# Casts, transfer order, working tiles and output queue in the opening of a linear-attention and mixer kernel

## The chip, the cores and the metric

The kernel runs on one core of a Trainium2 chip. A core has TensorE (PE, matrix multiply, with its weight loads shown as PEld), VectorE (DVE), ScalarE (ACT), GpSimd (POOL) and SyncE (SP), each with its own instruction stream, and 16 DMA engines. In this kernel SP and POOL issue the DMAs. The metric is the device time of one execution in microseconds; before the change its median over three runs is 300.36 us (299.21 to 301.64). One execution is also recorded by the hardware profiler; its times, counted from the start of its span, are the profile's.

## What is computed

Linear attention (elu + 1 feature map) over 8 batches of 8 heads, 576 tokens and 64 dimensions, and then an MLP mixer over tokens and channels on its result:

```python
def phi(x):
    return np.where(x > 0, x, np.exp(x) - 1.0) + 1.0
q_p, k_p = (phi(q), phi(k))                       # q, k, v: (8, 8, 576, 64) fp32
kv = np.einsum('bhsd,bhse->bhde', k_p, v)
z = np.sum(k_p, axis=2)
num = np.einsum('bhsd,bhde->bhse', q_p, kv)
den = np.einsum('bhsd,bhd->bhs', q_p, z)[..., None] + 1e-06
attn = num / den

x = attn.transpose(0, 2, 1, 3).reshape(8, 576, 512)
xt = x.transpose(0, 2, 1)
h = np.maximum(xt @ w_tok1, 0.0) @ w_tok2         # 576 -> 256 -> 576
u = x + h.transpose(0, 2, 1)
h2 = np.maximum(u @ w_ch1, 0.0) @ w_ch2           # 512 -> 1536 -> 512
out = u + h2                                      # (8, 576, 512) fp32
```

## The kernel before

**Tiling.** Of a batch's 576 tokens, 512 lie as 4 per partition on 128 partitions (index r = 0 to 3), and the last 64, the tail, as a fifth slot (r = 4) on half of the partitions: the lower half for even batches, the upper for odd ones. Two batches make a pair, so that one matmul of the channel mixer can take the tails of both. Heads come in two groups g of four. Inputs are loaded in fp32 into `*_raw` tiles, one set for even and one for odd batches.

**Steps of a batch.** `phi` makes phi(x) as max(min(exp(x), 1), x + 1): `phi_exp` on ACT (line 114), `phi_add` on DVE (line 120), and `phi_end` on DVE (lines 128 and 129) into `kp` or `qp`. `vcast` turns v to bf16 into `vs`, whose 65th column per head is one, so that `kv` (line 165) yields k'v and the sum of k' together; ACT copies these into `kvbd`. `qtr` transposes q' on PE (line 175), and ACT copies it into `qT`. `nd` multiplies both (line 196) and DVE divides into `x` (lines 206 to 209). `mm1` (line 231) and `mm2` (line 242) are the token mixer, DVE adds x to give `u` (line 248, the tail on line 246), `utr` transposes u (line 259). `mm3` (line 332) is the first channel matmul, 12 pieces of four matmuls, each followed by relu on ACT into `cr` (line 336), and `mm4` (line 355) the second, per tile t of tokens (0 to 3 and 4 to 7 of the pair's two batches, 8 for both tails), followed by an add on DVE into an output buffer (line 361) and a store (line 364). For batch 0 there are versions in two column halves (`mm1_first`, `mm2_first`, `utr_first`). `warm` issues matmuls of the identity whose result nobody reads.

**Order.** The schedule is by hand: each engine runs its instructions in the order in which the program issues them, and waits for data where it must. Buffers: a pool tile with `bufs=n` waits for its n-th predecessor's readers; `ps_big` has four PSUM banks, `ps_sm` two tiles of two banks, `outp` three output buffers, `work` two of each. After the opening, `run(bigs, fill)` walks through a list of big steps (mm3 and mm4 pieces of batch n) and after big step i issues the fill steps with number i (preparation of batches n+1 and n+2). Batch 0's mm4 (`m4_0`) goes through all four token tiles for each of the 12 slices kc of w_ch2, so w_ch2 is read slice by slice while its four slabs (three slices each) arrive.

**Transfers.** SP issues all loads of q, k, v and all stores. POOL issues the weights, which are converted to bf16 on the way: w_tok1 (`w1`, tail rows `w1t`), w_tok2 (`w2`), w_ch1 in four slabs (`wc1`, line 412) and w_ch2 in four slabs (`wc2`, line 417). `after(dma, other)` lets a DMA wait on its issuing engine until another has landed: w_tok1 waits for batch 0's last q, batch 1's k for the second w_ch1 slab, w_ch2's first slab for batch 1's first v, its second for batch 1's first q, and batch 2's k for w_ch2's third slab. Line numbers of the profile are those of the kernel before.

## Time and profile before

| | |
|---|---|
| median of 3 runs (lowest, highest) | 300.36 us (299.21, 301.64) |
| the profiled execution: its time, its span | 302.12 us, 300.3 us |
| granted TensorE clock, mean of the span | 0.988 |
| PE busy | 277.8 us (92%) |
| PEld busy (overlaps PE) | 158.5 us (53%) |
| DVE busy | 166.9 us (56%) |
| ACT busy | 167.4 us (56%) |
| POOL busy | 14.0 us (5%) |
| DMA | 41.84 MB, mean 139 GB/s |

A busy time is the time in which an engine executes; the span is the time from the first to the last event. An engine can be busy for a small share of the span and still decide it in one stage, so the views used below go by time: a table of busy times by stretch of the span, the timeline of instructions (with the idle time ahead of each and what ended it, in brackets), groups of instructions by line, and the chain of waits that ends last.

### The profile page before, as it was taken

To read this page: it belongs to the slowest core of one execution; us is meant where nothing else is said; L and a number is where in the kernel's file an instruction comes from. 1 tells how busy PE (TensorE), PEld (TensorE's weight loads), DVE (VectorE), ACT (ScalarE), POOL (GpSimd) and SP (SyncE) were. 2 spreads that over 40 slices of the span, in tenths; PEclk is the share of its full clock that TensorE was granted. 3 is DMA by queue.
4 is the path that set the end of the run, shared out by engine and by line. 5 is a ranking of instruction groups with operands and counts; after the bars stand their busy time and mean duration, and the time that the engine had idled before them with its cause. 6 is when DMAs were issued, how large, how long until landed. Compare 5 with 4: busy or idle time off the path is not lost.

```text
span 300.3 us, 5077 instructions
## 1 busy us (share of the span) xinstructions
PE 277.8 (92%) x1992; PEld 158.5 (53%) x1992; DVE 166.9 (56%) x324; ACT 167.4 (56%) x258; POOL 14.0 (5%) x24
## 2 busy tenths in 40 slices
PE   8968867976899989999999999999999999999994
PEld 8956324533374446545656455455565465454641
DVE  5794345646456794779276815595658617340021
ACT  3642688212997458655877437845797076126500
POOL 3190040000000000000000000000000000000000
PEclk9989999997999999999999999999999999999999
DMA  7969999997997595097308650011000210011022
GB/s 202 269 90 201 311 226 152 275 303 226 288 292 212 170 268 175 2 258 244 113 3 244 223 179 0 0 71 71 1 3 35 101 41 2 35 71 37 0 78 97
DMA packets 47959, 41.84 MB, mean 139 GB/s; under 512 B 14656, under 2 KB 43200, under 8 KB 47936
## 3 DMA queue, kind: packets, MB, share of 16 engines
q1 hardware_dynamic: 43648, 37.76, 43.3%
q0 software_dynamic: 4288, 3.77, 8.5%
q8 instruction: 15, 0.25, 0.3%
q14 instruction: 8, 0.07, 0.1%
HBM read 35.85 MB, written 9.44 MB: 151 GB/s over the span
## 4 chain that ended last, share of the span: by engine, by line
PE 70%; DMA 9%; ACT 7%; SPq 5%; DVE 3%; issue 2%; POOL 1%; ACTq 0%; DVEq 0%
PE h_ps L355 28%; PE c_ps L332 23%; PE a_ps L231 4%; PE h_ps L242 4%; SPq L105 3%; PE nd_ps L196 3%; PE c_ps L343 3%; DMA wc<-in_moe_w_ch_dram 3%; DMA v_raw<-in_v_dram 2%; PE tp L175 2%; ACT e L114 2%; PE tp L259 2%; SPq L103 2%; DMA q_raw<-in_q_dram 2%; PE kv_ps L165 2%
## 5 line engine op out<-in xcount | busy, mean ns | idle before, releaser
L332 PE MATMUL c_ps<-uT,wc 128*128 128x512 bf16 x384 | 93.8, 382 | 3.2 <-ACT cr L336 1.5
L355 PE MATMUL h_ps<-wc,cr 128*128 128x512 bf16 x384 | 90.4, 379 | 2.7 <-DMA wc<-in_moe_w_ch_dram 2.7
L336 ACT ACTIVATE cr<-c_ps 128x512 bf16<-128x512 f32 x96 | 56.8, 599 | 48.6 <-PE c_ps L332 48.4
L355 PEld LDWEIGHTS <-cr 128*128 128x128 bf16 x384 | 36.5, 98 | 42.5 <-DMA wc<-in_moe_w_ch_dram 3.2
L332 PEld LDWEIGHTS <-wc 128*128 128x128 bf16 x384 | 35.6, 98 | 37.2 <-issue 5.6
L128 DVE TENSOR_SCALAR e<-e 128x1280 bf16<-128x1280 bf16 (+1 forms) x34 | 17.0, 500 | 32.9 <-ACT e L114 32.9
L361 DVE TENSOR_TENSOR o_sb<-h_ps,u 128x512 f32<-128x512 f32 x32 | 21.8, 686 | 24.0 <-PE h_ps L355 20.0
L209 DVE TENSOR_TENSOR x<-nd_ps,den 128x512 bf16<-128x512 f32 (+1 forms) x48 | 28.9, 602 | 1.7
L206 DVE TENSOR_SCALAR den<-nd_ps 128x8 f32<-128x8 f32 (+1 forms) x48 | 7.8, 162 | 36.0 <-PE nd_ps L196 35.5
L263 ACT COPY uT<-tp 128x1024 bf16<-128x1024 bf16 x7 | 7.1, 1012 | 27.3 <-PE tp L259 27.3
L114 ACT ACTIVATE e<-k_raw 128x1280 bf16<-128x1280 f32 x16 | 20.3, 1270 | 3.4 <-DMA k_raw<-in_k_dram 3.3
L114 ACT ACTIVATE e<-q_raw 128x1280 bf16<-128x1280 f32 (+1 forms) x18 | 20.3, 1149 | 2.1 <-DMA q_raw<-in_q_dram 1.0
L196 PEld LDWEIGHTS <-qT 128*128 128x128 bf16 x160 | 13.0, 100 | 11.2 <-ACT qT L187 1.2
L187 ACT COPY qT<-tp 128x1280 bf16<-128x1280 bf16 x14 | 17.2, 1231 | 2.1 <-PE tp L175 2.1
L196 PE MATMUL nd_ps<-kvbd,qT 128*128 128x130 bf16 x160 | 17.4, 226 | 0.5 <-ACT qT L187 0.4
L248 DVE TENSOR_TENSOR u<-h_ps,x 128x1024 bf16<-128x1024 f32 x14 | 16.5, 1217 | 0.7 <-PE h_ps L242 0.7
L234 ACT ACTIVATE ar<-a_ps 128x512 bf16<-128x512 f32 x14 | 7.5, 592 | 15.7 <-PE a_ps L231 15.7
L242 PE MATMUL h_ps<-ar,w 128*128 128x512 bf16 x56 | 14.4, 379 | 0.8 <-ACT ar L234 0.7
L144 ACT CAST vs<-v_raw 128x1024 bf16<-128x1024 f32 x14 | 14.8, 1058 | 0.0
L385 PE MATMUL bank<-identity 128*128 128x128 bf16 x178 | 13.5, 247 | 1.4 <-POOL identity masks.py:199 1.4
L231 PE MATMUL a_ps<-x,w 128*128 128x512 bf16 x56 | 14.4, 379 | 0.0
L120 DVE TENSOR_SCALAR y<-k_raw 128x1280 bf16<-128x1280 f32 x16 | 13.2, 822 | 2.0 <-DMA k_raw<-in_k_dram 1.7
(76 smaller groups left out, 268.3 us busy)
## 6 DMA issues: line engine op xcount, KB each, us to landing
k_raw<-in_k_dram SPq DMA_DIRECT2D x16, 512.0 KB, 5.3
q_raw<-in_q_dram SPq DMA_DIRECT2D x16, 512.0 KB, 6.9
v_raw<-in_v_dram SPq DMA_DIRECT2D x16, 512.0 KB, 6.8
out_dram<-o_sb SPq DMA_DIRECT2D x32, 256.0 KB, 2.5
wc<-in_moe_w_ch_dram POOLq DMA_DIRECT2D x8, 384.0 KB, 8.0
k_raw<-in_k_dram SPq DMA_DIRECT2D x16, 64.0 KB, 5.2
q_raw<-in_q_dram SPq DMA_DIRECT2D x16, 64.0 KB, 6.5
v_raw<-in_v_dram SPq DMA_DIRECT2D x16, 64.0 KB, 6.4
```

What stands on the lines that cost most here:

```text
L114: nc.scalar.activation(out=e, in_=f, func=AF.Exp)
L128: nc.vector.tensor_scalar(out=e, in0=e, scalar1=1.0, scalar2=None, op0=ALU.min)
L187: nc.scalar.copy(out=qT[b][:, 2 * g:2 * g + 2].rearrange("p j r c -> p (j r) c"), in_=tp[:, 0:2 * R1])
L196: nc.tensor.matmul(out=ps[:, i, a * 2 * D1:(a + 1) * 2 * D1], lhsT=qT[b][:, j, r, :], rhs=kvbd[b][:, j, :], start=True, stop=True)
L209: nc.vector.tensor_tensor(out=x[b][:, rs[0]:rs[0] + m, HG * D * g:HG * D * (g + 1)].rearrange("p r (h d) -> p r h d", h=HG), in0=v_[:, :, ...
L231: nc.tensor.matmul(out=ps[:, mt], lhsT=w1t[:, b, ms] if r == R else w1[:, r, ms], rhs=x[b][:, r, :], start=(r == 0), stop=(r == R))
L242: nc.tensor.matmul(out=ps[:, i], lhsT=w2t[:, kt, b, :] if r == R else w2v[:, kt, r], rhs=ar[b][:, kt, :], start=(kt == 0), stop=(kt == NT ...
L248: nc.vector.tensor_tensor(out=u[b][:, rs[0]:rs[0] + m], in0=ps[:, 0:m], in1=x[b][:, rs[0]:rs[0] + m], op=ALU.add)
L332: nc.tensor.matmul(out=ps, lhsT=wc1[:, kj, 128 * mc:128 * mc + 128], rhs=uT[b][:, kj].rearrange("p r c -> p (r c)"), start=(kj == 0), stop ...
L336: nc.scalar.activation(out=cr[b][:, mc, :], in_=ps, func=AF.Relu)
L355: nc.tensor.matmul(out=ps, lhsT=crt[:, kc, :] if t == 8 else cr[b][:, kc, 128 * r:128 * r + 128], rhs=wc2[:, kc, :], start=(kc == 0), stop ...
L361: nc.vector.tensor_tensor(out=o, in0=ps, in1=ut[p % 2] if t == 8 else u[b][:, r, :], op=ALU.add)
```

## The change

- `vcast` of batch 0 runs on ACT and no longer on POOL; that of batch 1 runs on DVE.
- `kp`, `qp` and `vs` exist once and no longer for even and odd batches; v's tail slot becomes a tile of its own, `vst`, one for even and one for odd batches. `outp` has six buffers and the exponentials four.
- POOL's weight transfers follow w_tok1 at once. The second `w1t` part goes behind w_ch1, and w_ch2's first slab comes right behind that, without a wait; the other three wait for batch 1's last v. A wait on a load now means its main part, not its tail part.
- Stores go on POOL's queue, except those of the last pair, which stay on SP.
- In the opening both transposes of q of a head group go ahead of kv and nd (with copies on DVE for the first group); the fillers are placed anew (60, 20 of half width and 22 in the place of 130; 30 and 30 around a nd piece; some of 4 and 6). `mm2_first(1)` goes ahead of the first halves of mm3, of which there are two and no longer three.
- In batch 0's channel mixer `phi` of k is issued at steps 5 and 7 (8 and 9 before), `vcast` at 9 and 11 (11 and 12), kv at 11 (12), `phi` of q at 12 (14), the transposes at 14 and 15 (14 and 16), nd at 16 to 21 (17 to 22) and mm1 at 22 (23). The adds and stores of batch 0's four output tiles become `mm4_end`, issued after the sums u: the first ahead of `utr`, the others behind it.

The diff, cut to its core:

```diff
-    outp = ctx.enter_context(tc.tile_pool(name="outp", bufs=3))
+    outp = ctx.enter_context(tc.tile_pool(name="outp", bufs=6))
...
-    kp = [const(f"kp{b}", [128, R1, H, D]) for b in range(2)]
-    qp = [const(f"qp{b}", [128, R1, H, D]) for b in range(2)]
-    vs = [const(f"vs{b}", [128, R1, H, D1]) for b in range(2)]
+    kp = const("kp", [128, R1, H, D])
+    qp = const("qp", [128, R1, H, D])
+    vs = const("vs", [128, R, H, D1])
+    vst = [const(f"vst{b}", [128, H, D1]) for b in range(2)]
...
-        e = work.tile([128, HG * R1 * D], BF16, name="e", tag="e")[:, :nh * R1 * D]
+        e = work.tile([128, HG * R1 * D], BF16, name="e", tag="e", bufs=4)[:, :nh * R1 * D]
...
-    def vcast(n, g, eng=None):
+    def vcast(n, g, copy=nc.scalar.copy):
         b = n % 2
         hs = slice(HG * g, HG * g + HG)
-        dst = vs[b][:, 0:R, hs, 0:D].transpose([0, 2, 1, 3])
-        if eng is None:
-            nc.scalar.copy(out=dst, in_=raw["v", b][:, hs, 0:R])
-        else:
-            eng.tensor_copy(out=dst, in_=raw["v", b][:, hs, 0:R])
-        nc.scalar.copy(out=vs[b][half[b], R, hs, 0:D], in_=raw["v", b][half[b], hs, R])
+        copy(out=vs[:, :, hs, 0:D].transpose([0, 2, 1, 3]), in_=raw["v", b][:, hs, 0:R])
+        copy(out=vst[b][half[b], hs, 0:D], in_=raw["v", b][half[b], hs, R])
...
-        if put:
+        if put == "act":
             nc.scalar.copy(out=qT[b][:, j], in_=tp[:, 0:R1])
+        elif put == "dve":
+            nc.vector.tensor_copy(out=qT[b][:, j], in_=tp[:, 0:R1])
...
+    def mm4_end(p, t):
+        ps = held[t]
+        b, r = divmod(t, R)
         o = outp.tile([128, DM], FP32, name="o_sb", tag="o_sb")
         nc.vector.tensor_tensor(out=o, in0=ps, in1=ut[p % 2] if t == 8 else u[b][:, r, :],
                                 op=ALU.add)
+        put = nc.sync if p == B // 2 - 1 else nc.gpsimd
         if t < 8:
-            nc.sync.dma_start(
+            put.dma_start(
...
+    def warm_half(m):
+        ps = bank()
+        for i in range(m):
+            h = half[i % 2]
+            nc.tensor.matmul(out=ps[h, 0:D1], lhsT=identity[:, h], rhs=identity[:, 0:D1],
+                             start=True, stop=True)
...
     phi("k", 0, 0, HG)
-    warm(130)
+    warm(60)
+    warm_half(20)
+    warm(22)
     phi_exp("q", 0, 0, 2)
     phi_add("q", 0, 0, HG)
     phi_exp("q", 0, 2, 2)
-    vcast(0, 0, nc.gpsimd)
+    vcast(0, 0)
+    phi_end("q", 0, 0, 2)
+    phi_end("q", 0, 2, 2)
     for j in range(2):
-        phi_end("q", 0, 2 * j, 2)
-        qtr_pair(0, j, bank16(), True)
-    warm(8)
+        qtr_pair(0, j, bank16(), "dve")
+        warm(4)
     kv(0, 0, True)
-    warm(8)
+    warm(6)
     nd_mm(0, 0, [0, 1])
     nd_mm(0, 0, [2, 3])
 
     phi_exp("k", 0, HG, HG)
     phi_add("k", 0, HG, HG)
     nd_end(0, 0, [0, 1])
+    warm(30)
+    nd_mm(0, 0, [4])
+    warm(30)
     phi_end("k", 0, HG, HG)
     after(nc.gpsimd.dma_start(
         out=w1, in_=moe_w_tok1[0:SM, :].rearrange("(p r) t -> p r t", r=R)), landed["q", 1])
+    nc.gpsimd.dma_start(out=w1t[half[0], 0, :], in_=moe_w_tok1[SM:S, :])
+    nc.gpsimd.dma_start(out=w2, in_=moe_w_tok2.rearrange("(k p) s -> p k s", p=128))
+    c_in = [load_wc1(i) for i in range(NB)]
+    nc.gpsimd.dma_start(out=w1t[half[1], 1, :], in_=moe_w_tok1[SM:S, :])
+    c2_in = [load_wc2(0)]
     phi_exp("q", 0, 4, 2)
     phi_add("q", 0, 4, HG)
     phi_exp("q", 0, 6, 2)
-    vcast(0, 1, nc.gpsimd)
-    for b in range(2):
-        nc.gpsimd.dma_start(out=w1t[half[b], b, :], in_=moe_w_tok1[SM:S, :])
-    nc.gpsimd.dma_start(out=w2, in_=moe_w_tok2.rearrange("(k p) s -> p k s", p=128))
-    c_in = [load_wc1(i) for i in range(NB)]
-    warm(24)
+    vcast(0, 1)
     phi_end("q", 0, 4, 2)
+    qtr_pair(0, 2, bank16(), "act")
+    warm(4)
+    phi_end("q", 0, 6, 2)
+    qtr_pair(0, 3, bank16(), "act")
     kv(0, 1, True)
-    qtr_pair(0, 2, bank16(), True)
-    phi_end("q", 0, 6, 2)
-    qtr_pair(0, 3, bank16(), True)
-    nd_mm(0, 0, [4])
...
-    mm1_first(1)
+    mm1_first(1, range(R))
+    mm1_first(1, [R])
     utr_first(0)
-    for mc in range(3):
-        mm3(0, mc, range(0, 2))
     mm2_first(1, [0, 1], True)
     mm2_first(1, [2, 3], False)
+    for mc in range(2):
+        mm3(0, mc, range(0, 2))
     utr_first(1)
...
-    c2_in = [after(load_wc2(0), landed["v1", 0])]
     for g in range(2):
         landed["q1", g] = load("q", 1, g)
-    c2_in += [after(load_wc2(i), landed["q1", 0] if i == 1 else None) for i in range(1, NB)]
+    c2_in += [after(load_wc2(i), landed["v1", 1] if i == 1 else None) for i in range(1, NB)]
...
-    fill += [(8, lambda: phi("k", 1, 0, HG)), (9, lambda: phi("k", 1, HG, HG)),
-             (11, lambda: vcast(1, 0)), (12, lambda: vcast(1, 1)),
-             (14, lambda: phi("q", 1, 0, HG)), (14, lambda: phi("q", 1, HG, HG))]
-    fill += [(at0[nm], fn) for nm, fn in steps(1)]
+    fill += [(5, lambda: phi("k", 1, 0, HG)), (7, lambda: phi("k", 1, HG, HG)),
+             (9, lambda: vcast(1, 0, nc.vector.tensor_copy)),
+             (11, lambda: vcast(1, 1, nc.vector.tensor_copy))]
+    fill += [(at0[nm], fn) for nm, fn in steps(1) if nm[:2] == "kv"]
+    fill += [(12, lambda: phi("q", 1, 0, HG)), (12, lambda: phi("q", 1, HG, HG))]
+    fill += [(at0[nm], fn) for nm, fn in steps(1) if nm[:2] in ("qt", "nd", "mm")]
+    fill += [(23, lambda: mm4_end(0, 0))]
+    fill += [(at0[nm], fn) for nm, fn in steps(1) if nm[:2] == "ut"]
+    fill += [(23, lambda t=t: mm4_end(0, t)) for t in range(1, R)]
```

More of the change, by code (lines that the diff above doesn't have):

```diff
@@ L274, in sm_bank16, with mm1_first @@
         return ps_sm.tile([128, 2, 8, 128], BF16, name="bank216", tag="sm")[:, 0]
-    def mm1_first(g):
+    def mm1_first(g, rs):
         cs = COLS[g]
-        ps = (bank() if g == 0 else sm_bank()).rearrange("p (t c) -> p t c", t=NT)
+        if rs[0] == 0:
+            live["mm1"] = bank().rearrange("p (t c) -> p t c", t=NT) if g == 0 else ps_sm.tile(
+                [128, NT, 512], FP32, name="a_ps", tag="sm")[:, :, 0:DM // 2]
+        ps = live["mm1"]
         for mt in range(NT):
             ms = slice(128 * mt, 128 * mt + 128)
-            for r in range(R1):
+            for r in rs:
                 nc.tensor.matmul(out=ps[:, mt], lhsT=w1t[:, 0, ms] if r == R else w1[:, r, ms],
                                  rhs=x[0][:, r, cs], start=(r == 0), stop=(r == R))
-        nc.scalar.activation(out=ar[0][:, :, cs], in_=ps, func=AF.Relu)
+        if rs[-1] == R:
+            nc.scalar.activation(out=ar[0][:, :, cs], in_=ps, func=AF.Relu)
     def mm2_first(g, rs, add):
@@ L347, with mm4 @@
     held = {}
-    def mm4(p, t, kcs):
+    def mm4(p, t, kcs, wait=False):
         if kcs[0] == 0:
@@ L357, in mm4 @@
                 rhs=wc2[:, kc, :], start=(kc == 0), stop=(kc == NCH - 1))
-        if kcs[-1] < NCH - 1:
-            return
+        if kcs[-1] == NCH - 1 and not wait:
+            mm4_end(p, t)
+    def mm4_end(p, t):
+        ps = held[t]
+        b, r = divmod(t, R)
         o = outp.tile([128, DM], FP32, name="o_sb", tag="o_sb")
@@ L367, in mm4 @@
             for b in range(2):
-                nc.sync.dma_start(out=out[2 * p + b, SM:S, :], in_=o[half[b]])
+                put.dma_start(out=out[2 * p + b, SM:S, :], in_=o[half[b]])
     def prep_k(n, g):
@@ L464 @@
     nd_end(0, 1, [2, 3])
-    mm1_first(0)
+    mm1_first(0, range(R1))
     nd_mm(0, 1, [4])
```

35 lines of the change are left out of this document (18 added, 17 removed).

## The prediction

> **What bounds the kernel now.** I read the table by stretches first, cut where the character of the work changes, to see in which stretch TensorE (PE) is short of work. Its columns after the stretch are its length, the busy time of each engine with its count of instructions, the granted TensorE clock, the DMA share and GB/s.
>
> ```profile
> 0.00:28.09 28.09, 22.19 (x277) 20.56 (x278) 20.09 (x47) 12.97 (x21) 10.71 (x20) 0.94 0.89 190
> 28.09:45.43 17.34, 13.36 (x69) 6.19 (x68) 5.92 (x9) 11.58 (x21) 3.34 (x4) 1.00 1.12 258
> 45.43:72.40 26.97, 21.20 (x148) 11.85 (x149) 15.68 (x33) 9.95 (x15) 0.00 (x0) 0.98 0.93 234
> 72.40:110.06 37.66, 34.86 (x246) 18.80 (x245) 24.09 (x45) 26.93 (x40) 0.00 (x0) 0.97 0.93 253
> 110.06:296.29 186.23, 186.16 (x1259) 101.12 (x1256) 100.42 (x193) 105.96 (x163) 0.00 (x0) 1.00 0.28 85
> ```
>
> From 110.06 to 296.29 PE is busy 186.16 of 186.23 us at clock 1.00. Nothing in the change takes matmuls out of that stretch, so it can win nothing there; it could only lose. What can be won lies ahead of 110: PE is idle 5.9, 4.0, 5.8 and 2.8 us in the four earlier stretches, and some of its busy time runs at a lower clock. The table again, of PE alone, where the clock falls:
>
> ```profile
> 15.00:18.00 3.00, 1.17 (x21) 1.00 0.58 88
> 18.00:21.00 3.00, 1.98 (x24) 0.82 0.47 47
> 21.00:24.00 3.00, 2.95 (x22) 0.61 1.22 190
> 66.00:69.00 3.00, 0.53 (x3) 1.00 0.42 157
> 72.00:75.00 3.00, 3.00 (x13) 0.58 1.03 291
> ```
>
> There are two dips, each right after a stretch with little PE work. The first table row also shows the DMA at 88 and 47 GB/s from 15 to 21: the weights are not yet asked for. Then the timeline (start, length, engine, line, operation; in brackets the idle time before it and what ended it), first of the opening:
>
> ```profile
> 8.99 0.32 DVE L128 TENSOR_SCALAR e<-e 128x640 bf16<-128x640 bf16 x1
> 9.76 1.20 DVE L128 TENSOR_SCALAR e<-e 128x640 bf16<-128x640 bf16 x1
> 16.05 1.32 POOL L146 CAST vs<-v_raw 128x1024 bf16<-128x1024 f32 x1 [0.34 <-DMA v_raw<-in_v_dram]
> 16.48 1.57 DVE L120 TENSOR_SCALAR y<-q_raw 128x1280 bf16<-128x1280 f32 x1
> 17.42 0.73 PE L165 MATMUL bank<-vs,kp 128*128 128x130 bf16 x10 [1.83 <-POOL vs L146]
> 20.99 1.07 PE L196 MATMUL nd_ps<-kvbd,qT 128*128 128x130 bf16 x8
> 21.86 1.06 PE L282 MATMUL bank<-x,w 128*128 128x256 bf16 x4
> 25.60 0.60 PE L282 MATMUL bank<-x,w 128*128 128x256 bf16 x4
> 28.09 1.46 PE L332 MATMUL c_ps<-uT,wc 128*128 128x512 bf16 x6 [0.78 <-DVE uT L311]
> 29.38 0.38 PE L292 MATMUL bank<-ar,w 128*128 128x256 bf16 x2
> 32.60 1.70 PE L332 MATMUL c_ps<-uT,wc 128*128 128x512 bf16 x6 [0.67 <-ACT uT L313]
> ```
>
> One VectorE (DVE) instruction takes 1.20 us where its twin takes 0.32, and another 1.57, both while a GpSimd (POOL) cast runs; PE waits 1.83 us for that cast; and the same four matmuls of line 282 take 1.06 us in the first dip and 0.60 out of it. Batch 0's middle and batch 1's opening, in the same view:
>
> ```profile
> 34.77 7.93 PE L332 MATMUL c_ps<-uT,wc 128*128 128x512 bf16 x36
> 42.56 2.59 POOL L417 DMA_DIRECT2D wc<-in_moe_w_ch_dram  x3 [3.31 <-DMA q_raw<-in_q_dram]
> 45.43 1.04 PE L355 MATMUL h_ps<-wc,cr 128*128 128x512 bf16 x4 [2.72 <-DMA wc<-in_moe_w_ch_dram]
> 48.60 2.43 ACT L114 ACTIVATE e<-q_raw 128x1280 bf16<-128x1280 f32 x2
> 51.31 0.73 PE L175 MATMUL tp<-identity,qp 128*128 128x128 bf16 x10 [1.61 <-DVE qp L129]
> 53.60 0.72 PE L175 MATMUL tp<-identity,qp 128*128 128x128 bf16 x10
> 61.36 1.03 PE L231 MATMUL a_ps<-x,w 128*128 128x512 bf16 x4
> 67.31 0.69 DVE L361 TENSOR_TENSOR o_sb<-h_ps,u 128x512 f32<-128x512 f32 x1 [3.98 <-DMA out_dram<-o_sb]
> 69.18 0.59 PE L242 MATMUL h_ps<-ar,w2t 128*128 128x512 bf16 x2 [2.65 <-DVE u L248]
> 72.40 9.27 PE L332 MATMUL c_ps<-uT,wc 128*128 128x512 bf16 x36
> ```
>
> Three waits carry the loss: 2.72 us for the first w_ch2 slab, 1.61 for batch 1's q, and a chain that ends at 69.18: the fourth output buffer (three exist) waits 3.98 us for a store, the sums u stand behind it on DVE, and PE waits 2.65 for them. The 36 matmuls after it take 9.27 us, where 36 equal ones took 7.93: the second dip cost 1.34.
>
> **The change part by part.** I follow the start of four pieces of work on PE and say how much earlier each comes.
>
> *Opening, to the second halves of mm3 (32.60 now).* Without POOL casts DVE gets 0.88 us back at 9.76 and 0.74 at 16.48. The casts go to ACT. These groups by line (count, busy time, mean ns) price them and the later moves:
>
> ```profile
> L144 ACT CAST vs<-v_raw 128x1024 bf16<-128x1024 f32 x14 | 14.8, 1058 | 0.0
> L120 DVE TENSOR_SCALAR y<-k_raw 128x1280 bf16<-128x1280 f32 x16 | 13.2, 822 | 2.0 <-DMA k_raw<-in_k_dram 1.7
> L248 DVE TENSOR_TENSOR u<-h_ps,x 128x1024 bf16<-128x1024 f32 x14 | 16.5, 1217 | 0.7 <-PE h_ps L242 0.7
> L311 DVE COPY uT<-bank 128x1024 bf16<-128x1024 bf16 x1 | 0.7, 691 | 0.8 <-PE bank L308 0.8
> ```
>
> On ACT the first cast fits between the q exponentials and the kv copies, since the two qT copies of that group go to DVE, at between nothing and 0.69 us each (line 311, a wider copy). The second can start only when v lands (POOL began it at 16.05), so it ends at about 17.4, its small tail soon after. By then DVE, 0.6 us ahead and not slowed, has q's halves at 17.5 and 18.3. In the new order PE transposes both, does kv, and reaches the numerator matmuls at about 20.0 against 20.99: 1.0 us. The fillers of 30 sit in the hole from 15 to 18 that went ahead of the first dip, so the clock should stay up: the matmuls at 20.99 and 21.86 alone run about 0.45 us too long each now, and the pieces to mm2_first gain 0.8 us more, 1.8 in sum. Last, mm2_first(1) no longer stands behind mm3's six half matmuls and their 0.78 us wait; those become four, and cover the wait for u instead: another 1.6. The second halves of mm3 begin near 29.2, 3.4 us earlier. (The 20 half-width fillers are taken at nothing: they end before the first q is ready.)
>
> *To batch 1's kv.* PE has 44 matmuls of mm3 left and two of the token tail, at 7.93/36 us each: it is through at 29.2 + 10.1 = 39.3. Batch 1's transfers hang on the second w_ch1 slab, in the chain of waits (start, length):
>
> ```profile
> 20.12 7.75 DMA wc<-in_moe_w_ch_dram
> ```
>
> It is asked for behind the cast and two issues; in the new order it follows w_tok1 directly, some 2.3 us earlier (1.32 of the cast, its waits, one w1t issue), lands near 25.6 against 27.87, and releases k then. The w_ch2 slab put behind it takes some 2 us of the DMA (0.39 MB written at the 190 GB/s of the row from 21 to 24). k and v of batch 1 are 2.36 MB, 8.1 us at the 291 GB/s of the row from 72 on; behind 2 us for the rest of w_ch1 and 2 for that slab, v ends near 37.5 and k four us before it. That is enough: exp(k) is now emitted at steps 5 and 7, 22 and 30 matmuls on, near 34.0 and 35.8. The v casts move from ACT to DVE: between 0.66 us (822 ns times 1024/1280) and ACT's 1.06; I take 0.66, plus 0.16 for the tail's 256 elements, since line 120 reads the same type on the same engine. From an exponential's start to PE's use of it are 51.31 - 48.60 = 2.7 us now, so DVE ends k's second half at about 38.8 (ACT's queue adds 0.3) and the casts at 39.6 and 40.4; kv follows there, m4 starts at 41.1 and finds its slab, landed by about 30 to 32. The 2.72 us wait is gone; what is late next is v's cast, for about 1.0 us in two pieces.
>
> *To the end of q's second transposes (54.3 now).* ACT has lost two casts there, 2.1 us and their tails. But w_ch2's slabs 1 to 3 are now released by v and not by q, so q shares the DMA with them. Now the gate on q opens at 42.56, so q's last piece is there by some 42 to 43. Alone, q's 1.18 MB take 4.0 us from 37.5 on; sharing evenly with the slabs they end near 45.5; with all three slabs ahead (6 us) near 47.5. I take 45.5, since queues of one core that both have work have to share the same 16 engines. The same 2.7 us from exponential to transposes and 0.1 to reach it put these at 48.3 to 48.9. That is 5.4 us earlier, with one m4 step fewer done ahead of it. Behind the exponential that waits on ACT stands the first qT copy, needed only after the next step; slab 1 lands at about 46 while PE asks at 45, inside the same wait.
>
> *To batch 1's mm3 (72.40 now).* The seven steps between second transposes and mm1 are the same number: 61.36 - 54.3 = 7.1, so mm1 at 56.0. From mm1 to mm3 it takes 72.40 - 61.36 = 11.0 now. With mm1 one step earlier, m4's last step of 0.86 us covers the wait for relu; without the store wait u follows at once (two sums of 1.22), the tail sum, one output sum of 0.69, and uT (0.69 a copy on line 311): 8.3 with PE's own work between. What is late next is the second uT copy, behind that output sum, for 0.3 us, counted in. So mm3 starts near 64.3: 8.1 us earlier. The second dip, worth 1.34, should go with the hole; PE still has gaps of 0.5 to 0.9 us there, so I take 1.0.
>
> [...]
>
> *The rest.* Single kp, qp and vs tiles make the producer of batch n+2 wait for the reader of n+1; the loops put kv and the transposes at steps 0 to 3 and the producers at 10 and later, so I take nothing, with 0.5 us a batch as the end if a wait appeared. Storing from POOL frees SP's queue: batch 3's loads no longer stand behind four stores. From 72.40 on PE is idle for 2.8 us in all, whatever it waits for, so I take nothing here. The last pair stays on SP, so the end is unchanged.
>
> Sum: 8.1 + 1.0 = 9.1 us. The profiled execution took 302.1 us (span 300.3 and 1.8 around it), so 293.0; the median of the runs is 1.8 lower, and in its terms the forecast is 300.4 - 9.1 = 291.3.
>
> **The rivals.** *Transfers set the pace.* If the second w_ch1 slab still lands at 27.87 and w_ch2's first pushes k and v back by 2 us, v ends near 40, q near 48; the second transposes end at about 51.6 instead of 54.3. That gives 2.7 us, and the last part's 2.7 and 1.0 remain: 6.4, so 294.0. For it: DMA shares of 1.12 and 0.93 in the middle stretches. Against: 88 and 47 GB/s from 15 to 21, which is room.
>
> *More than forecast.* q lands as early as now, so PE does not wait at the second transposes (1.5 us), and half of the 2.8 us idle from 72.40 to 110.06 goes as the loads come earlier: 288.4.
>
> *Stores on POOL slow DVE in every later batch, and it ends slower.* A POOL cast cost DVE 0.74 to 0.88 us. Batches 0 to 5 store from POOL, four or five times each; sums u and PE's transposes follow each other closely there. If it were like the cast, up to 4 us a batch could be lost. Below (9.1 - 3.0)/6 = 1.0 us of PE idle a batch the change stays faster by over 1%; from (9.1 + 3.0)/6 = 2.0 on it is slower by over 1%; at 2.5 us it is 300.4 - 9.1 + 15 = 306. Against it: four POOL issues leave a DVE operation beside them as long as its mean.
>
> ```profile
> 19.37 3.00 POOL L412 DMA_DIRECT2D wc<-in_moe_w_ch_dram  x4
> 19.92 0.69 DVE L209 TENSOR_TENSOR x<-nd_ps,den 128x512 bf16<-128x512 f32 x1
> L209 DVE TENSOR_TENSOR x<-nd_ps,den 128x512 bf16<-128x512 f32 x32 | 22.1, 691 | 1.1
> ```
>
> [...]
>
> **How the numbers follow.** Forecast 0.58 (291.3), transfers 0.20 (294.0), more 0.08 (288.4), stores on POOL 0.14: of this 0.04 a loss under 1.0 us a batch, 0.05 within 1%, 0.05 slower. The range runs from 287 to 298; outside are part of the better case and most of the last one. Within 1% (297.4 to 303.4, about what this kernel's runs can tell from no change) I add 0.04 and for slower 0.01 for faults I don't name, taken from the forecast. Faster 0.58 + 0.20 + 0.08 + 0.04 - 0.05 = 0.85, same 0.09, slower 0.06.
>
> **What would show it.** Right: no DVE minimum over 0.5 us in the opening; clock 1.00 from 18 to 24 and after 60; numerator matmuls of line 196's second group near 20; mm3's second halves near 29; no wait for w_ch2 ahead of the first m4; transposes of batch 1's q near 48.5, with ACT waiting on q's DMA; no DVE wait for a store; batch 1's mm3 near 64; and then 227 us to the end of the span. Wrong: k or v of batch 1 landing after 38, PE idle after 110, or DVE sums longer beside stores.

## The result, and the profile after

The changed kernel takes 292.68 us (median; 292.12 to 294.02). The kernel before took 301.0 us beside it (median of four, one more than the three of its first series). The ratio of the means is 0.974 with a 95% interval of 0.968 to 0.980: faster by 2.6%. The forecast was 291.3, in a range from 287 to 298. The profiled execution took 292.58 us with a span of 290.8. Two single executions of the experiments below, of 1015.94 and 325.45 us, lie far from the rest of their series and are left out of all figures.

First the table of busy times by stretch of the kernel after, cut at the same pieces of work as in the prediction but for the last cut, which is the start of batch 2's mm3, and then its PE alone where the clock had fallen before (length, PE, PEld, DVE, ACT, POOL with counts, clock, DMA share, GB/s):

```profile
0.00:28.36 28.36, 23.53 (x309) 21.20 (x310) 19.99 (x50) 14.55 (x23) 9.50 (x19) 1.00 0.99 206
28.36:41.30 12.94, 11.80 (x66) 5.62 (x66) 7.29 (x12) 9.70 (x20) 1.22 (x2) 1.00 1.13 291
41.30:63.61 22.31, 19.22 (x132) 10.06 (x130) 14.05 (x29) 7.62 (x9) 1.25 (x3) 1.00 1.07 249
63.61:101.92 38.31, 35.52 (x255) 19.33 (x253) 27.26 (x51) 28.30 (x41) 5.38 (x8) 1.00 0.96 284
101.92:286.50 184.58, 184.34 (x1249) 100.29 (x1247) 99.11 (x190) 104.49 (x161) 11.98 (x22) 1.00 0.27 84
...
21.00:24.00 3.00, 2.51 (x24) 1.00 1.28 195
72.00:75.00 3.00, 1.68 (x8) 1.00 1.09 286
```

The clock is 1.00 in every row. PE is idle 4.8, 1.1, 3.1 and 2.8 us in the first four stretches, against 5.9, 4.0, 5.8 and 2.8. In the last PE is as good as full, as it was: 184.34 of 184.58 us, before 186.16 of 186.23 from a cut 1.7 us earlier in the work.

The timeline of the kernel after, at the places that the prediction named:

```profile
9.91 0.32 DVE L130 TENSOR_SCALAR e<-e 128x640 bf16<-128x640 bf16 x1
15.54 0.83 DVE L122 TENSOR_SCALAR y<-q_raw 128x1280 bf16<-128x1280 f32 x1
19.69 0.62 PE L196 MATMUL nd_ps<-kvbd,qT 128*128 128x130 bf16 x8 [0.21 <-ACT kvbd L167]
28.36 2.13 PE L336 MATMUL c_ps<-uT,wc 128*128 128x512 bf16 x8 [0.67 <-ACT uT L317]
...
33.99 0.83 DVE L122 TENSOR_SCALAR y<-k_raw 128x1280 bf16<-128x1280 f32 x1 [2.35 <-DMA k_raw<-in_k_dram]
39.48 0.40 PE L163 MATMUL kv_ps<-vs,kp 128*128 128x130 bf16 x4 [0.79 <-DVE vs L144]
41.30 2.75 PE L359 MATMUL h_ps<-wc,cr 128*128 128x512 bf16 x12
43.84 1.27 ACT L116 ACTIVATE e<-q_raw 128x1280 bf16<-128x1280 f32 x1 [0.24 <-DMA q_raw<-in_q_dram]
45.04 0.73 PE L173 MATMUL tp<-identity,qp 128*128 128x128 bf16 x10 [0.98 <-DVE qp L131]
47.16 0.73 PE L173 MATMUL tp<-identity,qp 128*128 128x128 bf16 x10 [0.53 <-DVE qp L131]
...
54.93 1.03 PE L231 MATMUL a_ps<-x,w 128*128 128x512 bf16 x4
60.55 0.59 PE L242 MATMUL h_ps<-ar,w2t 128*128 128x512 bf16 x2 [0.45 <-DVE u L248]
63.61 8.21 PE L336 MATMUL c_ps<-uT,wc 128*128 128x512 bf16 x36
73.32 1.89 PE L336 MATMUL c_ps<-uT,wc 128*128 128x512 bf16 x8 [1.50 <-ACT cr L340]
```

The minimum takes 0.32 us where it took 1.20, the add 0.83 where it took 1.57. The first m4 step has no wait ahead of it, where 2.72 us for its slab stood; the wait of 2.65 us for u is 0.45. New are the waits for the v cast (0.79, and 0.23 at the second) and for q (0.98 and 0.53).

### The profile page after: what moved, and what is told of

It is laid out like the page before. It is cut to its first block, busy times and chain, and to the rows that moved or that the text cites. A ratio compares the mean times of both kernels' runs of the same rounds, so it can differ in the third digit from the quotient of the medians.

```text
span 290.8 us, 5019 instructions
## 1 busy us (share of the span) xinstructions
PE 274.4 (94%) x2002; PEld 156.5 (54%) x2002; DVE 168.2 (58%) x329; ACT 164.7 (57%) x254; POOL 29.3 (10%) x52
## 4 chain that ended last, share of the span: by engine, by line
PE 72%; DMA 11%; SPq 5%; ACT 4%; DVE 3%; issue 2%; POOL 1%; ACTq 0%
PE h_ps L359 28%; PE c_ps L336 22%; DMA q_raw<-in_q_dram 7%; PE a_ps L231 5%; PE h_ps L242 4%; DMA wc<-in_moe_w_ch_dram 3%; SPq L106 3%; PE nd_ps L196 3%; PE c_ps L347 3%; SPq L104 2%; PE tp L173 2%; PE tp L259 2%; PE kv_ps L163 2%; ACT e L116 2%; DMA k_raw<-in_k_dram 1%
## 5 line engine op out<-in xcount | busy, mean ns | idle before, releaser
L336 PE MATMUL c_ps<-uT,wc 128*128 128x512 bf16 x384 | 92.8, 379 | 2.4 <-ACT cr L340 1.5
L373 POOL DMA_DIRECT2D out_dram<-o_sb x24 | 14.4, 601 | 164.1 <-DVE o_sb L369 142.3
L130 DVE TENSOR_SCALAR e<-e 128x1280 bf16<-128x1280 bf16 (+1 forms) x34 | 16.1, 474 | 22.0 <-ACT e L116 22.0
L248 DVE TENSOR_TENSOR u<-h_ps,x 128x1024 bf16<-128x1024 f32 x14 | 16.5, 1218 | 4.8 <-PE h_ps L242 4.8
L196 PE MATMUL nd_ps<-kvbd,qT 128*128 128x130 bf16 x160 | 16.8, 221 | 0.9 <-ACT kvbd L167 0.5
```

The lines of the kernel that those rows point to most:

```text
L130: nc.vector.tensor_scalar(out=e, in0=e, scalar1=1.0, scalar2=None, op0=ALU.min)
L196: nc.tensor.matmul(out=ps[:, i, a * 2 * D1:(a + 1) * 2 * D1], lhsT=qT[b][:, j, r, :], rhs=kvbd[b][:, j, :], start=True, stop=True)
L248: nc.vector.tensor_tensor(out=u[b][:, rs[0]:rs[0] + m], in0=ps[:, 0:m], in1=x[b][:, rs[0]:rs[0] + m], op=ALU.add)
L336: nc.tensor.matmul(out=ps, lhsT=wc1[:, kj, 128 * mc:128 * mc + 128], rhs=uT[b][:, kj].rearrange("p r c -> p (r c)"), start=(kj == 0), stop ...
```

## The experiments

The theory was the prediction's: many small waits ahead of batch 1's mm3 go, each by its own part of the change. The rivals were that the transfers alone set the pace there, that one part (the output buffers) brings nearly all of it, and that stores on POOL's queue cost time that hides in the sum.

Each ratio below is to the kernel before, run beside that series (medians 300.15, 300.8 and 300.41 us). A run that puts one part back is read against the change itself, which in two series of executions had the medians 292.68 and 293.7 and lay between 292.05 and 294.57.

The spread goes with the clock. Of these ten executions the six with a mean granted clock of 0.996 or more took 292.05 to 293.17 us, and the four with 0.986 to 0.993 took 294.02 to 294.57. Where a median alone is too coarse, like is compared with like by this.

**The output buffers alone, on the kernel before.** To make room for a fourth buffer, `qp` exists once in this run.

```diff
-    outp = ctx.enter_context(tc.tile_pool(name="outp", bufs=3))
+    outp = ctx.enter_context(tc.tile_pool(name="outp", bufs=4))
...
-    qp = [const(f"qp{b}", [128, R1, H, D]) for b in range(2)]
+    qp = const("qp", [128, R1, H, D])
```

> The kernel before with a fourth output buffer; to make room for it qp exists once, and nothing else is changed. By the sum: DVE no longer waits 3.98 us for a store at 63, the sums u come 2.6 us earlier, PE's hole of 2.65 us ahead of the token tail goes and with it the clock's second dip (1.34 us): 3.6 to 4.0 us less than the kernel before, mm3 of batch 1 near 69.8 instead of 72.4, clock 1.00 after it. If the dip belongs to something else than that hole, 2.6 us less and the dip stays. If the wait was hidden behind the other adds or turns into a wait on a transfer, within 1 us of the kernel before. If the single qp tile makes a wait, DVE waits on PE's transposes at line 129 and the gain is smaller by it.

Measured: 300.3 us (298.64 to 301.88) against 300.15, ratio 0.9996 (0.9968 to 1.0024). The gain failed to come. The store wait was gone. The timeline of this run, and then its PE by stretch:

```profile
45.50 1.89 PE L355 MATMUL h_ps<-wc,cr 128*128 128x512 bf16 x4 [3.69 <-DMA wc<-in_moe_w_ch_dram]
62.93 1.03 PE L231 MATMUL a_ps<-x,w 128*128 128x512 bf16 x4
71.61 2.75 PE L332 MATMUL c_ps<-uT,wc 128*128 128x512 bf16 x12
```

```profile
0.00:31.70 31.70, 24.55 (x301) 1.00 0.92 198
45.50:61.36 15.86, 15.21 (x100) 0.82 1.05 237
```

From mm1 to mm3 it takes 8.68 us (71.61 - 62.93) in place of 11.04, and the second dip is gone (clock 1.00 from 72 to 75). But the wait for w_ch2 is 3.69 us, and a dip of the clock comes with it (0.82 in the mean from 45.50 to 61.36). The slab came no later than in the first profile (m4 starts at 45.50, there at 45.43). PE only got to it 0.9 us sooner, since the opening of this execution has no dip, though its code is that of the kernel before. Either the wait had been moved, or the execution that the prediction read was unlike most. The next run asks that.

**The kernel before, profiled once more.** No edit.

> The kernel before once more, for a second profile of it. The fourth buffer alone left the median where it was although its own profile shows the hole at 63 to 69 gone. If the profile before was one of its slow executions, this one has a shorter wait of the fourth output buffer for a store (under 2 us instead of 3.98) or only one dip of the clock, and a span of about 298.5. If that profile is typical, the wait is again near 4 us with two dips, span about 300, and the missing gain of the fourth buffer has another cause.

This execution took 298.82 us, span 297.0. Its timeline, and its PE by stretch:

```profile
44.59 1.04 PE L355 MATMUL h_ps<-wc,cr 128*128 128x512 bf16 x4 [1.88 <-DMA wc<-in_moe_w_ch_dram]
65.18 0.69 DVE L361 TENSOR_TENSOR o_sb<-h_ps,u 128x512 f32<-128x512 f32 x1 [1.84 <-DMA out_dram<-o_sb]
67.05 0.59 PE L242 MATMUL h_ps<-ar,w2t 128*128 128x512 bf16 x2 [0.52 <-DVE u L248]
70.33 1.89 PE L332 MATMUL c_ps<-uT,wc 128*128 128x512 bf16 x8
```

```profile
21.00:24.00 3.00, 2.95 (x21) 0.60 1.28 193
72.00:75.00 3.00, 3.00 (x15) 1.00 1.08 300
```

The first dip is there again. The store wait is 1.84 us and not 3.98, PE waits 0.52 for u and not 2.65, and there is no second dip. So most of the 2.7 and 1.0 us that the prediction set on the store wait and the dip behind it belongs to the execution that was profiled, and not to every one. That fits the run before: it took away a wait that costs about 0.3 us (8.96 - 8.68) in this execution. The first store was issued at 62.15 and 62.16, and DVE's wait for it ended at 67.31 in the first profile and at 65.18 in this one. SP had issued the last of batch 2's loads ahead of it by 61.25 in the one and by 58.72 in the other (in the first they land 6.2 to 7.4 us after their issue), and from 63 to 66 the DMA moved 329 GB/s in the one and 278 in the other. So in the first profile the stores had late loads beside them on the DMA. Why the loads were late in the one, the runs do not show.

**All stores back on SP's queue.**

```diff
-        put = nc.sync if p == B // 2 - 1 else nc.gpsimd
+        put = nc.sync
```

> The changed kernel with all stores on SyncE's queue, as in the kernel before; six output buffers stay. By the sum the queue of the stores is worth nothing: within 0.5 us of the changed kernel (292.7), milestones up to 64 us unchanged; batch 3's loads then stand behind four stores and start near 66 instead of 57, without anybody waiting for them. If stores on GpSimd's queue slow VectorE, this is faster by 1 us or more, and the adds beside stores get shorter. If freeing SyncE's queue was what paid, it is slower by 2 us or more.

Measured: 292.49 us (291.69 to 293.93), within the spread of the change. The sums of DVE by line in this run, with its stores (count, KB, us from issue to landing), and then both of the change:

```profile
L248 DVE TENSOR_TENSOR u<-h_ps,x 128x1024 bf16<-128x1024 f32 x14 | 16.5, 1218 | 4.8 <-PE h_ps L242 4.8
```

```profile
out_dram<-o_sb SPq DMA_DIRECT2D x32, 256.0 KB, 2.5
```

```profile
L248 DVE TENSOR_TENSOR u<-h_ps,x 128x1024 bf16<-128x1024 f32 x14 | 16.5, 1218 | 4.8 <-PE h_ps L242 4.8
```

```profile
out_dram<-o_sb POOLq DMA_DIRECT2D x24, 256.0 KB, 2.9
```

DVE's sums take as long with stores on POOL as without (1218 ns). A store from POOL takes 0.4 us longer to land (2.9 for 2.5), and no wait for one stands among the waits of the change. The rival that stores on POOL slow DVE falls. A difference of 0.5 us at the end of the program remains and is taken up in the last section.

**Casts on POOL and the break in the weights put back.** These two belong together: the casts stand in POOL's queue between the weights. Each cast's small tail stays on ACT, and the second group's q exponentials go ahead of the weights with the cast.

```diff
-    vcast(0, 0)
+    vcast(0, 0, nc.gpsimd.tensor_copy)
...
+    phi_exp("q", 0, 4, 2)
+    phi_add("q", 0, 4, HG)
+    phi_exp("q", 0, 6, 2)
+    vcast(0, 1, nc.gpsimd.tensor_copy)
...
-    phi_exp("q", 0, 4, 2)
-    phi_add("q", 0, 4, HG)
-    phi_exp("q", 0, 6, 2)
-    vcast(0, 1)
```

> The changed kernel with batch 0's two large v casts back on GpSimd, in front of w1t, w2, w_ch1 and w_ch2's first slab as in the kernel before; the rest stays. By the sum the casts and the break in the weights cost 1.0 us on the path to the numerator matmuls (20.7 instead of 19.7) and delay the second w_ch1 slab and batch 1's k by about 2 us (28 instead of 25.7); since k landed at 34.0 just when ACT asked for it, the exponentials of k then stand behind it on ACT: 2 to 3 us more in all, with a DVE minimum over 1 us again. If the cost was only the contention on VectorE, 0.5 to 1 us more. If transfers set the pace and their order moves nothing, k still lands near 34 and the time is within 0.5 us.

Measured: 294.85 us (293.74 to 295.85), ratio 0.982 (0.978 to 0.986). Its timeline:

```profile
16.07 1.60 POOL L144 CAST vs<-v_raw 128x1024 bf16<-128x1024 f32 x1 [0.79 <-DMA v_raw<-in_v_dram]
16.78 1.57 DVE L122 TENSOR_SCALAR y<-q_raw 128x1280 bf16<-128x1280 f32 x1
36.56 0.83 DVE L122 TENSOR_SCALAR y<-k_raw 128x1280 bf16<-128x1280 f32 x1 [3.00 <-DMA k_raw<-in_k_dram]
41.99 0.40 PE L164 MATMUL kv_ps<-vs,kp 128*128 128x130 bf16 x4 [1.39 <-DVE vs L144]
```

The add beside the second cast is back at 1.57 us, k lands 2.6 us later, and kv of batch 1 starts 2.5 us later. Beside the first cast it is the product into `qp` (line 131) that takes 1.21 us in place of 0.49, and PE waits 0.81 for it. Batch 1's mm3 starts at 66.40, 2.8 us later, where the medians show about 1 to 2. Of the 2.8 us, 1.9 are there at mm3's second halves (30.27). The clock is at half there from 12.15 to 15.56, which also happens in runs without these casts, so the casts' own share of the 1.9 is not separated.

**Without the two groups of 30 fillers.**

```diff
-    warm(30)
     nd_mm(0, 0, [4])
-    warm(30)
```

> The changed kernel without the two groups of 30 filler matmuls around the numerator piece r = 4 of the first head group; the work that counts is the same. By the sum these keep the clock up through the hole: without them the clock falls between 17 and 24 and the opening takes 1.0 to 1.8 us longer to mm2_first, about 1 to 1.5 us in the end. [...] If the dip of the kernel before came from elsewhere, nothing changes, and the fillers are idle weight.

Measured: 294.62 us (293.07 to 296.15), ratio 0.980 (0.975 to 0.985). Timeline and PE by stretch of this run:

```profile
22.13 1.07 PE L196 MATMUL nd_ps<-kvbd,qT 128*128 128x130 bf16 x8
31.95 2.13 PE L336 MATMUL c_ps<-uT,wc 128*128 128x512 bf16 x8 [0.67 <-ACT uT L317]
```

```profile
12.00:15.00 3.00, 2.65 (x26) 0.62 0.77 211
21.00:24.00 3.00, 3.00 (x26) 0.50 1.20 173
```

The dip from 18 to 24 is back and the numerators take 1.07 us again. The 3.6 us that this profile is late at mm3's second halves are not the fillers' alone: a dip that begins ahead of them, at 10.87, belongs to it. Against the two medians of the change the fillers are worth 0.9 to 1.9 us.

**The first halves of mm3 ahead of mm2_first(1) again.**

```diff
+    for mc in range(2):
+        mm3(0, mc, range(0, 2))
...
-    for mc in range(2):
-        mm3(0, mc, range(0, 2))
```

> The changed kernel with the first halves of mm3 again ahead of mm2_first(1), as in the kernel before; there are two halves, not three. By the sum this order is worth 1.6 us: mm2_first(1) waits for uT again, and the second halves of mm3 begin near 30.0 instead of 28.4; all of it should reach the end, since kv has only 0.8 us of slack there. If the wait for u only changes place, under 0.5 us.

Measured: 294.59 us (293.88 to 295.23), ratio 0.980 (0.978 to 0.983). The time is read inside the opening: mm3's second halves start 10.05 us after the second group's numerators (30.82 - 20.77), in the change 8.67 (28.36 - 19.69). The order is worth 1.4 us there, for the 1.6 expected.

**The first w_ch2 slab behind batch 1's v again.**

```diff
-    c2_in = [load_wc2(0)]
...
+    c2_in = [after(load_wc2(0), landed["v1", 0])]
```

> The changed kernel with w_ch2's first slab again issued after batch 1's first v has landed, as in the kernel before; nothing else moves. By the sum the slab then comes near 42 to 44 (asked for at about 35 to 36, 7 to 8 us to land), m4 waits 1 to 3 us for it at 41.3, and k and v land 1.5 to 2 us earlier (32 and 36): 0.5 to 2 us slower. If it is the transfers that set the pace, k and v come 2 us earlier, kv at 38.5 and the time is the same or up to 1 us less. In no case more than 3 us slower.

Measured: 294.88 us (293.71 to 295.24), ratio 0.981 (0.976 to 0.986). The timeline of this run:

```profile
36.19 0.76 POOL L433 DMA_DIRECT2D wc<-in_moe_w_ch_dram  x1 [16.18 <-DMA v_raw<-in_v_dram]
42.82 2.43 ACT L116 ACTIVATE e<-q_raw 128x1280 bf16<-128x1280 f32 x2
44.28 1.90 PE L359 MATMUL h_ps<-wc,cr 128*128 128x512 bf16 x8 [2.06 <-DMA wc<-in_moe_w_ch_dram]
```

PE waits 2.06 us for the slab, but ACT no longer waits for q: the transfers only change places. From mm3's second halves to batch 1's mm3 it takes 35.68 us (64.73 - 29.05) against 35.25 (63.61 - 28.36), so of a wait of 2.06 us only 0.4 reach the end of that stretch. All four executions of this run have a mean clock of 0.990 to 0.994; their median lies 0.6 us above that of the change's four with a clock as low (294.24).

**Slabs 1 to 3 gated on q again.**

```diff
-    c2_in += [after(load_wc2(i), landed["v1", 1] if i == 1 else None) for i in range(1, NB)]
+    c2_in += [after(load_wc2(i), landed["q1", 0] if i == 1 else None) for i in range(1, NB)]
```

> The changed kernel with w_ch2's slabs 1 to 3 again released by batch 1's first q and not by its last v. By the sum q then has the DMA to itself and lands 1.5 to 2 us earlier (no wait of ACT for q after 41, transposes at 45.0 and 46.3 instead of 45.0 and 47.2), but the second slab, asked for near 41, comes only at 47 to 49 where PE wants it at 45.6: 1 to 3 us slower. If sharing with the slabs had cost q nothing, q lands as now and only the slab's wait is added. If q's landing was the pace there, 0.5 us faster.

Measured: 294.31 us (294.25 to 295.47, three executions), ratio 0.980 (0.975 to 0.985). The timeline of this run:

```profile
41.25 2.70 POOL L433 DMA_DIRECT2D wc<-in_moe_w_ch_dram  x3 [20.78 <-DMA q_raw<-in_q_dram]
44.00 2.43 ACT L116 ACTIVATE e<-q_raw 128x1280 bf16<-128x1280 f32 x2
47.28 1.03 PE L359 MATMUL h_ps<-wc,cr 128*128 128x512 bf16 x3
```

No wait for slab 1 stands ahead of 47.28, so a wait for it does not take the place of the one for q. From mm3's second halves to batch 1's mm3 it takes 35.03 us (65.28 - 30.25): in this execution the gate costs nothing there. PE still waits 0.72 and 0.53 us ahead of q's transposes though ACT no longer waits for q, so in the change, too, most of the 0.98 and 0.53 is ACT's and DVE's own work on q and not its transfer. This profile is 1.9 us late ahead of that, in the opening, which the edit does not touch; its clock fell there, and its mean is 0.992. But the other two executions, with clocks of 0.998 and 0.999, took 295.47 and 294.31 us, 1.1 us or more above every execution of the change with a clock that high. They have no trace, so whether the gate costs 1 to 3 us in them, as the sum had it, stays open.

**Batch 1's v casts on ACT again.**

```diff
-             (9, lambda: vcast(1, 0, nc.vector.tensor_copy)),
-             (11, lambda: vcast(1, 1, nc.vector.tensor_copy))]
+             (9, lambda: vcast(1, 0)),
+             (11, lambda: vcast(1, 1))]
```

> The changed kernel with batch 1's v casts back on ScalarE, at the same steps. By the sum VectorE's casts are cheap (0.7 us and 0.3) and ScalarE's dear, since relus and exponentials queue there: two casts with tails are 2.9 us of ScalarE between 36 and 42, kv comes at 41 to 42 instead of 39.5 and q's first exponential at about 43.5 instead of 42.3; 1.0 to 2.0 us slower. If q's landing sets the pace there, under 0.5 us slower, since q's second half lands at 43.8 anyway.

Measured: 294.52 us (293.83 to 295.88), ratio 0.981 (0.977 to 0.984). PE's two waits ahead of kv in this run's timeline:

```profile
40.28 0.39 PE L163 MATMUL kv_ps<-vs,kp 128*128 128x130 bf16 x4 [1.37 <-ACT vs L144]
42.91 0.39 PE L163 MATMUL kv_ps<-vs,kp 128*128 128x130 bf16 x4 [1.70 <-ACT vs L144]
```

3.07 us in place of 1.02 (0.79 and 0.23). Batch 1's mm3 starts at 65.73, in the change run beside it at 64.16; 0.4 of these 1.6 us come from the opening. That leaves 1.2 us, in the expected 1.0 to 2.0.

**Batch 2's v casts on DVE too.** The wait of 1.50 us at 73.32 stands in a stretch where ACT is the bound: from 70 to 80 it is busy 9.92 us of 10, with casts of batch 2 between the relus.

```diff
-        vcast(n, g)
+        vcast(n, g, nc.vector.tensor_copy if n == 2 else nc.scalar.copy)
```

> The changed kernel with batch 2's v casts on VectorE and no longer on ScalarE. From 70 to 80 ScalarE is busy 9.92 us of 10 and VectorE 5.92, and PE waits 1.50 us for a relu at 73.3; two casts with tails are 2.9 us of ScalarE. If that wait is what the casts cause, PE's wait goes and the time falls by 1.0 to 1.5 us. If VectorE's chain of k and q becomes the bound there, kv waits for its casts (0.7 and 0.3 us each) and the gain is under 0.5 us or a loss of 0.5.

Measured: 290.58 us (289.77 to 291.36), ratio 0.966 (0.963 to 0.970): the best of all, below every execution of the change. The same stretch in this run and then in the change:

```profile
70.00:80.00 10.00, 9.89 (x114) 7.33 (x115) 6.95 (x12) 9.90 (x19) 0.00 (x0) 1.00 1.12 312
```

```profile
70.00:80.00 10.00, 8.50 (x94) 5.97 (x93) 5.92 (x9) 9.92 (x19) 0.00 (x0) 1.00 1.03 297
```

PE does 114 matmuls there instead of 94. From batch 1's mm3 to batch 2's it takes 35.9 us (99.33 - 63.44) instead of 38.3, 2.4 us, more than the 1.0 to 1.5 expected and than the casts' wait of 1.50 that the profile names. PE's idle time in that stretch falls from 2.8 to 1.15 us (the wait for qT of 0.35 us at 83.37 goes too), and its busy time by 0.8.

**The same with 36 fillers in the place of 22 ahead of q's first transposes.**

```diff
-    warm(22)
+    warm(36)
```

> The kernel of batch 2's casts on VectorE, with 36 fillers in the place of the 22 ahead of q's first transposes. The 60 fillers at the start take 4.8 to 6.4 us in the profiles so far, as the clock comes up early or late, and the idle time after the fillers is 0.4 to 2.3 us; where it is 1.8 or more, the clock falls at about 12 and the opening is 0.7 to 1.9 us later. If that idle time causes the fall, 14 more fillers (0.9 us) take the late executions away: spread of the runs under 1 us, median 0.3 to 0.8 us under the 290.6 of batch 2's casts alone, clock 1.00 from 9 to 15. If the fall has another cause, same median and spread. If the fillers run into the transposes, 0.3 to 0.5 us slower where the clock comes up late.

Measured: 290.73 us (290.07 to 292.76, five executions), ratio 0.968 (0.965 to 0.971). No gain over the run without them, and no smaller spread. In its profile PE has no gap ahead of the transposes, and the clock is 1.00 from 9 to 15.

**The change once more, as a control.** No edit.

> The changed kernel once more, as the mark for the three beside it: 292.1 to 294.0 us, median near 292.7, the slower executions with a clock that falls ahead of 15 us.

Measured: 293.7 us (292.05 to 294.57), ratio 0.977 (0.974 to 0.979). Numerators at 19.53, mm3's second halves at 28.20, mm1 at 55.48, batch 1's mm3 at 64.16: its milestones lie within 0.6 us of the change's first profile.

## Why the prediction was right, and where not

The start of each piece of work, in us, and what the change gained up to there against both profiles of the kernel before:

| | before | before again | after | gain against the one, the other | forecast |
|---|---|---|---|---|---|
| mm3's second halves | 32.60 | 32.61 | 28.36 | 4.24, 4.25 | 3.4 |
| mm1 of batch 1 | 61.36 | 61.37 | 54.93 | 6.43, 6.44 | 5.4 |
| mm3 of batch 1 | 72.40 | 70.33 | 63.61 | 8.79, 6.72 | 8.1 |
| mm3 of batch 2 | 111.79 | 108.46 | 101.92 | 9.87, 6.54 | 9.1 |
| last sum on DVE | 296.29 | 292.96 | 286.30 | 9.99, 6.66 | 9.1 |
| the execution | 302.12 | 298.82 | 292.58 | 9.54, 6.24 | 9.1 |

**The time.** Against the profile that it was made from the sum was nearly met: 9.5 for 9.1. Against the median it was too much: 300.36 - 292.68 = 7.7, or 8.3 from the 301.0 measured beside it. The prediction took the sum of one execution, which lay 1.8 us above the median, off the median. The step that failed is "without the store wait ... 8.3", and with it the second dip, "I take 1.0". Of 11.04 us between mm1 and mm3, 2.1 belonged to that one execution (8.96 in the other), and so did the dip. After the change this stretch takes 8.68 us, so the term of 2.7 was 2.4 against the one profile and 0.3 against the other, and the dip's 1.0 was 1.1 and nothing. Columns one and two of the table show it: they agree to 0.01 us up to mm1 and differ by 3.3 at batch 2. The run with the buffers alone has the same 8.68 us and no gain in the median. The executions of the kernel before between 299 and 303 us leave room for both kinds; how often each comes, two profiles cannot tell. That 292.68 is only 1.4 us from the forecast is in part luck: up to mm1 the sum was 1.0 us too small, and the two terms behind it were too large by up to 3.6.

**The opening** was under-sized: 4.2 for 3.4. Numerators at 19.69, for 20.0. The order gives 1.4, for 1.6. The dip gives 0.9, for 0.8: the buffers-alone run, without that dip, had the second halves at 31.70. What is left, 0.6 us, has no row of its own.

**To batch 1's kv** m4 came at 41.30, for 41.1, though mm3 was 0.8 ahead: the exponentials of k stand 5.7 us behind mm3's second halves (34.04), not 4.8. They did not wait for k, which landed just in time (DVE's add waits for it up to 33.99); where it landed earlier, in the run with the slab late, they stand at the same distance (34.74 - 29.05). "v's cast, for about 1.0 us in two pieces" is 0.79 and 0.23. Three groups of the kernel after give the casts and copies on DVE (count, busy time, mean ns):

```profile
L144 DVE CAST vs<-v_raw 128x1024 bf16<-128x1024 f32 x2 | 1.4, 694 | 0.0
L145 DVE CAST vst<-v_raw 64x256 bf16<-64x256 f32 x2 | 0.7, 350 | 0.1
L179 DVE COPY qT<-bank 128x640 bf16<-128x640 bf16 x2 | 1.0, 488 | 0.1
```

The cast is 0.69, for 0.66; its tail 0.35, for 0.16. The qT copy is 0.49, inside its bounds.

**q** landed by 43.84, for 45.5: in this execution an even share of the DMA with the slabs was too hard a view, and "with all three slabs ahead (6 us)" is out. The second transposes end at 47.9 and not at 48.9. But the price of 2.72 us set on the slab's wait was only right inside the chain: taken back alone the slab's place costs 2.06 us of waiting and 0.4 of time, since then q comes sooner. DMA shares of 1.13 and 1.07 in the two stretches go with that.

**The rivals.** *Transfers set the pace* gave 294.0, and the control's median of 293.7 is nearer to that than to 291.3, so the time alone does not decide. But its conditions did not come in (second transposes end at 47.9, not 51.6), though a seed of it is right, as the slab shows. *More* had neither condition quite: q came at 43.84, between the 42 to 43 of before and the 45.5 of the forecast, and PE still waits 0.53 us at the second transposes. PE is still idle for 2.8 us in the fourth stretch, 1.5 of them at 73.32 for ACT. *Stores on POOL slow DVE* is refuted at 1218 ns with and without. What is behind the 0.4 us more of landing no run here shows, and DVE's sums pay nothing for it. *Single tiles* cost nothing: from batch 2's mm3 to the last sum it takes 184.50 us before (296.29 - 111.79) and 184.38 after (286.30 - 101.92). A single tile also made the room for the buffer in the first experiment, a use that the prediction did not name.

**The clock.** The 1.0 that the prediction took for the second dip and the whole 1.34 that it read (9.27 - 7.93) cannot be told apart here. The granted clock is 1.00 from 66 to 75 after; the 36 matmuls take 8.21 us against 9.27, but the second profile of before had no such dip to remove.

## What to carry to other kernels

Before a wait for a DMA is priced, profile the kernel a second time: here one store wait was 3.98 us in one execution and 1.84 in the next, and the terms hanging on it were 3.7 of 9.1 us. In the stretches filled with transfers here (DMA shares of 1.13 and 1.07) a wait that went for one came back for another, so price the stretch and not the wait (2.06 us of wait, 0.4 of time). And look for the engine that is busy 9.9 of 10 us: one line that moved two casts off it was worth 2.1 us between the medians (3.1 from the control's), as much as any single part tested here.

## What the runs showed of the hardware that was not expected

**In these profiles the clock's changes lie multiples of 3.41 us apart, and it fell after 3.41 us with 0.66 to 1.78 us of work.** Ahead of q's first transposes PE has a gap whose length differs between executions, since the first 60 fillers take from 4.78 to 6.36 us. That the clock comes up early or late there, as the forecast of the run with 36 fillers has it, is not shown: the granted clock is 1.00 from 0 to 9 us in the change, with the slab late and with q's gate, where they take 6.01, 5.21 and 4.89. Where the gap was 1.77 us (the slab late) or 2.31 (q's gate; no fillers), the granted clock was 0.50, 0.58 and 0.62 from 12 to 15; it also fell (at 12.15) in the run with the casts back, where two gaps of 1.45 and 0.81 us follow each other. With gaps of 0.42 to 1.68 us in six profiles of the changed kernel and its variants, and none in a seventh, it did not fall there. PE in the run with the slab late:

```profile
9.00:12.00 3.00, 1.79 (x27) 0.96 1.12 316
12.00:15.00 3.00, 3.00 (x30) 0.50 0.90 232
```

The length of the gap alone does not sort these cases: in the first profile of before a gap of 2.72 us (ahead of 45.43) brought no fall (clock 1.00 from 45 to 48). The table of busy times in steps of 0.02 us gives the moments at which the clock changes:

| profile | clock falls at | PE busy in the 3.41 us ahead | clock is back at |
|---|---|---|---|
| before | 19.91 | 1.46 | 23.32 |
| before | 71.11 | 1.27 | 74.52 |
| before again | 20.01 | 1.78 | 23.43 |
| buffers alone | 44.51 | 0.70 | 51.34 |
| casts back | 12.15 | 1.36 | 15.56 |
| no fillers | 10.87 | 1.10 | 14.28 |
| no fillers | 17.70 | 0.66 | 24.53 |
| slab late | 11.76 | 1.55 | 15.17 |
| gate on q | 11.10 | 1.02 | 14.51 |

Within each of these seven profiles all changes lie a whole number of 3.41 us apart (from 19.91 to 71.11 it is 15 of them). So one can lay borders 3.41 us apart through them. Cut like that, the first profile of before has PE busy for 1.46 and 1.27 us in the two stretches at full clock that end in a fall, and for 1.78 or more in all others from 2.84 to 129.14. The two ranges overlap between profiles: a stretch with 1.78 us ended in a fall in the second profile of before, and one with 1.61 (from 42.48) in none with the slab late. The fallen clock was back after one stretch where PE was busy for 3.3 us or more in it, and after two where it was 2.42 and 2.38 in the first. The gap of 2.72 us has a border in it, at 43.80, with 2.31 us of work on its one side and 1.78 on the other. The opening with the buffers alone has the gap of 1.83 us ahead of 17.4 as the first profile has it, but its borders lie elsewhere: 1.82 and 2.15 us of work, and no fall. So that opening came with a fall and without one. With the fillers of 30 PE is busy 2.44 of 3.00 us from 15 to 18 after the change, and the clock is 1.00 from 18 to 24 in all seven profiles that have these fillers and were read there.

The gap ahead of q's first transposes is new with the change: with the 130 fillers of before PE is busy 2.85 to 3.00 of 3.00 us from 9 to 12, in three profiles. In the openings with the slab late and with q's gate, where the clock fell, mm3's second halves start 0.7 and 1.9 us later than in the change (29.05 and 30.25 for 28.36), and the change's executions with a mean clock of 0.986 to 0.993 are its four longest. The run with 36 fillers in the place of 22 has no gap there in its profile, but gained nothing that can be measured.

**With stores on POOL's queue the program ended 0.5 us later after its last sum.** From the start of the last sum on DVE to the end of the span it takes 4.5 us in four profiles where batches 0 to 5 store from POOL, and 4.0 in four where all stores go from SP, though the last pair is on SP in all. Among executions with a mean clock of 0.996 or more the median is 292.13 us with all stores on SP (five) and 292.6 in the change (six), which fits, but the two overlap. Why the end is later was not tried.
